# H3 block with a feed-forward branch on one Trainium2 core: another order around the first layer norms, two rows on GpSimd, another estimate for transposing transfers

## The chip, the cores and the metric

The kernel runs on one core of a Trainium2 chip. The metric is the device time of one execution, in microseconds (us). The engines of the core are named as in the profile: PE is TensorE (matmuls; PEld its weight loads), DVE is VectorE, ACT is ScalarE, POOL is GpSimd, SP is SyncE, which issues most of the transfers. Each engine works off its own queue of instructions in order; semaphores order the engines among each other.

## The reference

The input has S = 2048 rows of D = 1024 numbers; the feed-forward width is F = 3584. All inputs and the output are float32.

```python
def reference(q, k, v, shift_k, ssm_k, ssm_D, x, w1, w2):      # x of the branches is q
    xn = layernorm(q)                                          # per row, eps 1e-5
    k_shift = causal depthwise conv of k with 4 taps (shift_k)
    kv = k_shift * v
    y = irfft(rfft(kv, 2S) * rfft(ssm_k, 2S))[:S] + kv * ssm_D # per channel, over the rows
    return q + xn * y + silu(xn @ w1) @ w2
```

This is pseudocode of the reference, cut to what matters. The input `x` of its signature is not read; the two matrix products of the last term are most of the work.

## The kernel before

**Matrix products.** TensorE multiplies float16. Each float32 operand is split into a high and a low float16 part (`split`, L365): ScalarE writes the high part (L355), VectorE the low part (L347), and three matmuls per tile (high times high, high times low, low times high: L930 to L932 for the first product, L1062 to L1064 for the second) give nearly float32. The feed-forward products use a scheme with seven products of blocks in place of eight (as Strassen's): sums of blocks, named S1 to S4 for the activations and T1 to T4 for the weights, are made on VectorE ahead of the split. A few "plain" column blocks at the start (pairs 0 and 1 of w1) are done without these sums, so that TensorE has work early.

**The start.** Rows come in as 16 tiles `xt` of 128 x 1024 (128 rows of the input, one to a partition). `ln_rows` (L485) takes them in groups: tiles 0 and 1, 2 and 3, 4 to 7, then the last eight. For each group VectorE collects statistics (L497, L499), ScalarE takes a square root, VectorE forms 1/std (L503 to L507) and applies the norm in place, one `tensor_scalar` over 128 x 1024 a tile (L516). `transposes` (L527) has TensorE transpose the rows 512 columns at a time into PSUM (tile `ft`, L535), and `first_rows`, `lower_sums` (L585) and `upper_sums` make from them the operands A11, A12, A21, A22 and S1 to S4 in eight places of SBUF. `x_rows` (L623) holds this together: first the plain rows A11 and A12 of tiles 0 to 3, then A21, A22 and S1 of tiles 4 to 7 (`lower_sums`), then S2, S3, S4 (`upper_sums`). S4's place is the place in which the raw weights of pair 1 lie until they are split. In before, `x_rows` waits for the places of A22, S2, S3, S1 and S4, in this order, ahead of the first `lower_sums`.

The weights are scaled by powers of two. `scales_w1` (L706) has ScalarE sum the squares (tile `junk`), one small matmul adds them over the partitions (`norm`, L441), and VectorE forms the scales `wsc`; `factors_w1` (L747) then splits the weights into the tiles `wo`. `warm_up` (L1788) puts 26 small matmuls without a use at TensorE's start.

**The convolution.** It is done channel group by channel group (128 channels, eight groups g0 to g7), among the feed-forward matmuls. ScalarE and VectorE make `acc`, the signal k_shift * v. `signal_parts` (L1470) splits a quarter of it at a time into the tile `cm` (ring `cm_r`, one buffer, in part of the kernel also `ht`); `parts_of` (L1481) issues on SP a transposing transfer from it into the tile `hl` (helper `X`, L334). `stage1` (L1501) is the forward transform as matmuls (L1529 to L1531), ScalarE and VectorE take its result into `spec`, VectorE multiplies the spectra and does the inner transforms (tiles `spec`, `tmp`), the result is split into `zh` and `zl`, and `stage1_inv` (L1707, matmuls L1721 to L1723) transforms back. `gated` (L1729) multiplies with the normed row on VectorE into a tile `yt`, or, at the end of the kernel, into a half of a `wo` buffer, and adds it to the output in memory with two accumulating transfers that GpSimd issues (helper `G`, L339). The feed-forward results are added the same way (`out<-hf`); the last ones are written by SP.

**What sets the order.** All instructions are emitted by a planner (class `Order`, L106) while the program is built; the chip then runs fixed queues. The parts of the kernel are streams (generators) that yield operations. An operation carries its engine, an estimate of the time for which it holds the engine (`busy`), how long after that its result can be read (`late`), what it reads and writes, and a margin that is added to the time at which its operands are there. Among the next operations of all streams the planner emits the one with the least planned start less the stream's bias. Of a transfer it assumes that it ends no earlier than 3.0 us after its issue plus its bytes at 330 KB a us plus 0.2, one after the other, and no earlier than issue + busy + late. Where TensorE is planned to wait (after a planned 45 us), it emits dummy matmuls (`fill`). An activation with another function table than the one before it is charged 1.28 us. So a number in an estimate changes no operation, only the place in each engine's queue in which operations come out, and with it which buffers they get. All buffers are rings of fixed places; an operation that needs a place is emitted only when the planner has already emitted the last use of what is in it.

Of the kernel before, what the change touches and what calls it, by code (L numbers as in the profile page):

```python
# [13 lines left out]
F16 = mybir.dt.float16  # L14
I32 = mybir.dt.int32
AF = mybir.ActivationFunctionType
ALU = mybir.AluOpType
AX = mybir.AxisListType
ADD, SUB, MUL = ALU.add, ALU.subtract, ALU.mult

P = 128
# [6 lines left out]
KH = KD // 2  # L28
# [12 lines left out]
XPLACE = dict(A11=2, A12=3, A22=5, S1=0, S2=6, S3=7, S4=1)  # L41
# [64 lines left out]
class Order:  # L106
# [27 lines left out]
    def add(self, gen, bias, floor=0.0):  # L134
        s = Stream(gen, bias, floor)
        self.streams.append(s)
        self.advance(s)
# [154 lines left out]
def h3_ffn_kernel(ctx, tc, x, kp, vs, fs, shift, dskip, w1, w2, cfwd, cinv, out):  # L292
    nc = tc.nc
    ctx.enter_context(tc.manual_schedule())
    order = Order()
    add = order.add
    flag = defaultdict(Token)
# [18 lines left out]
    def V(f, o, ins, us=None, m=0.15):  # L316
        return Op("DVE", us or 1.03 * (size(o) / 960 + 0.075), 0.16, f, ins, [o], m)
# [16 lines left out]
    def X(o, i, m=0.3):  # L334

        n = size(o) * o.shape[0] * mybir.dt.size(o.dtype)
        return Op("SP", 0.6, 0.1, lambda: nc.sync.dma_start(o, i, transpose=True), [i], [o], m, n)

    def G(o, i, m=0.3):  # L339
        n = size(i) * i.shape[0] * mybir.dt.size(i.dtype)  # L340
# [135 lines left out]
    def load_row(t):  # L476
# [5 lines left out]
            yield L(xts[t][0][:, q], xr[t // T2, t % T2][:, q])  # L482
        flag["xt", t].set()

    def ln_rows():  # L485
        for t0, n, bias in ((0, 2, 0.26), (2, 2, 0.17), (4, 4, 0.15), (8, 8, 0.03)):
            yield bias
            q = slice(t0, t0 + n)
            mv = lnp.tile([P, 2, 8], F32, name="mv", bufs=2)
            m = mv[:, :, 0:n]  # L490
            order_in = (8, 9, 12, 13, 10, 11, 14, 15) if n == 8 else range(t0, t0 + n)
            for t in order_in:
                yield flag["xt", t]
                xt = xts[t][0]
                st = lnp.tile([P, 2, 6], F32, name="st", bufs=2)
                for a in range(2):
                    yield V(lambda: nc.vector.bn_stats(st[:, a, :], xt[:, a * W:(a + 1) * W]), st[:, a, :],  # L497
                            [xt[:, a * W:(a + 1) * W]], us=0.65)
                yield V(lambda: nc.vector.bn_aggr(stat[:, t, :], st), stat[:, t, :], [st], us=0.2)  # L499

            def chain(m=m, q=q):
                v = stat[:, q, 1]
                nc.vector.reciprocal(m[:, 0, :], m[:, 0, :])  # L503
                nc.vector.tensor_mul(m[:, 1, :], m[:, 0, :], m[:, 0, :])
                nc.vector.scalar_tensor_tensor(m[:, 1, :], v, 1e-5, m[:, 1, :], op0=ADD, op1=MUL)
                nc.vector.tensor_scalar(m[:, 1, :], m[:, 1, :], -0.5, 1.5, op0=MUL, op1=ADD)
                nc.vector.tensor_mul(rstd[:, q], m[:, 0, :], m[:, 1, :])  # L507
                if n == 8:
                    nc.vector.scalar_tensor_tensor(nmr, stat[:, :, 0], -1.0, rstd, op0=MUL, op1=MUL)
            yield a_act(m[:, 0, :], stat[:, q, 1], AF.Sqrt, bias=eps)  # L510
            p = V(chain, rstd[:, q], [stat[:, q, :], m[:, 0, :]], us=0.8)
            p.writes += [m[:, 0, :], m[:, 1, :]] + ([nmr] if n == 8 else [])
            yield p
            for t in order_in:
                xt = xts[t][0]
                yield V(lambda: nc.vector.tensor_scalar(xt, xt, stat[:, t, 0:1], rstd[:, t:t + 1], op0=SUB, op1=MUL),  # L516
                        xt, [xt, stat[:, t, :], rstd[:, t:t + 1]], us=0.78)
                flag["xn", t].set()

    pts = []  # L520
# [102 lines left out]
    def x_rows():  # L623
        yield from first_rows()
        second["A21"], second["tok"] = places[4].tile([P, 4, KH, 2, P], F16)
        for name in ("A22", "S2", "S3", "S1", "S4"):
            r = places[XPLACE[name]]
            yield r.ready
            xo[0][name], xtok[0][name] = r.tile([P, 4, KH, 2, P], F16)

        class Kept:
            bias = 0.14

            def __init__(self, i):
                self.i = i

            def __call__(self, name):
                if name in ("A11", "A12"):
                    return None
                o = (second["A21"] if name == "A21" else xo[0][name])[:, self.i]  # L640
                return lambda src, tok: split(o[:, :, 0], o[:, :, 1], src, XS, (tok, flag["x", 0, name]))

        yield 0.14
        half = []
        for i in range(4):
            half.append((yield from lower_sums(Kept(i), s1_r)))
        Kept.bias = 0.11
        yield 0.11
        for i in range(4):
            yield from upper_sums(Kept(i), xst_r, *half[i], t=i)  # L650

        class Spilled(Kept):
            bias = 0.02

            def __call__(self, name):
                return None if name == "A21" else lambda src, tok: spill(xsp[name][:, self.i], src, tok)

        def spill(o, src, tok):
            yield lambda: s1_r.ready() or xst_r.ready()
            r = s1_r if s1_r.ready() else xst_r  # L660
            st, stok = r.tile([P, KH, 2, P], F16)
            yield from split(st[:, :, 0], st[:, :, 1], src, XS, (tok,))
            yield L(o, st)
            stok.set()
            flag["spilled"].set()

        yield 0.02
        for i in range(4):
            part = yield from lower_sums(Spilled(i), sums_r)
            yield from upper_sums(Spilled(i), sums_r, *part)  # L670
        flag["x done"].set()
# [34 lines left out]
    def scales_w1():  # L706
        for n, (_, i) in enumerate(pairs):
            yield (0.25, 0.16, 0.1, 0.05)[min(n, 3)]
            m = 4 if n == 0 else 2
            if n >= NP:  # L710
                for a in range(m):
                    yield flag["raw", n, a]
                flag["scaled", n].set()
                continue
            yield sq_r.ready
            ss, tok = sq_r.tile([P, 4])
            for a in range(m):
                yield flag["raw", n, a]
                r = raws[n][2][a]
                yield a_act(junk[:, 0:r.shape[1]], r, AF.Square, total=ss[:, a:a + 1])  # L720

            def then(e, i=i):
                sc = wsc[:, i]
                nc.vector.tensor_scalar(sc[:, 3:5], powers[:, 3:5], e, None, op0=MUL)
                nc.vector.reciprocal(e, e)
                nc.vector.tensor_scalar(sc[:, 0:3], powers[:, 0:3], e, None, op0=MUL)
            yield from norm(ctxs["nm"], ss[:, 0:m], (m,), then, ([wsc[:, i]], [flag["scaled", n], tok]))

    spills = []

# [1067 lines left out]

    warm = lnp.tile([P, 1], F32, name="warm")
    nc.scalar.activation(warm, ones[:, 0:1], AF.Sqrt)  # L1800
    add(begin(), 0.05)
    add(warm_up(), 0.0)
    add(x_rows(), 0.03)
# [53 lines left out]
```

## Time and profile before

| | us |
|---|---|
| median of 3 runs | 1257.72 |
| lowest and highest | 1257.01, 1260.42 |
| profiled execution, its time | 1257.19 |
| profiled execution, span from the first to the last instruction | 1255.4 |
| busy: TensorE, VectorE, ScalarE, GpSimd | 1233.6, 1147.3, 731.0, 132.6 |

The mean granted clock of TensorE is 0.996. In the rows of the profile, L355 stands for all ScalarE operations of the helper `a_act`, L347 and L344 for VectorE's helpers `v_stt` and `v_tt`; so a row is read by its tiles (out<-in) rather than by its line. A row of a timeline gives the start, the duration, the engine and line, the operation with its tiles and shapes, and in brackets how long the engine was idle ahead of it and what ended that wait. A matmul's row is longer than the distance to the next one, since matmuls overlap.

### The profile page before, as it was taken

Reading aid. Unit: us, or ns where it says so; the run is one execution under the profiler, and the core shown is the slowest. Engines: PE = TensorE matmul, PEld = TensorE weight load, DVE = VectorE, ACT = ScalarE, POOL = GpSimd, SP = SyncE. Lnnn points to the kernel's source line nnn. Section 1 sums busy time; section 2 is a strip of 40 time slices with the busy share of each in tenths; the row PEclk is TensorE's granted clock in tenths of the full one; section 3 lists DMA queues with packets and bytes.
Section 4 is the critical chain, followed back from the end, with each engine's and each line's share of the span. In section 5 each row is a group of like instructions: output and inputs, shape, how many; then the busy total and the mean of one; then the engine's idle time right before and its main releaser. Section 6 shows DMA issues by size and latency. Waiting matters only on the chain.

```text
span 1255.4 us, 17118 instructions
## 1 busy us (share of the span) xinstructions
PE 1233.6 (98%) x6058; PEld 599.7 (48%) x6058; DVE 1147.3 (91%) x1517; ACT 731.0 (58%) x1165; POOL 132.6 (11%) x141
## 2 busy tenths in 40 slices
PE   7999999999999999999999999999999999899998
PEld 6544554444444544445444544544454454345444
DVE  7999997999899979999999899989989979898994
ACT  6868887878767776748752632463173264426222
POOL 0000000000000020002010300210030030113114
PEclk9999999999999999999999999999999999999999
DMA  9358889889999998879998887699597578978777
GB/s 334 94 185 293 288 297 315 285 278 325 337 335 281 264 286 262 267 224 239 352 316 209 168 270 180 147 265 263 116 220 172 129 171 245 227 157 140 163 143 92
DMA packets 254293, 292.93 MB, mean 233 GB/s; under 512 B 48768, under 2 KB 167808, under 8 KB 252032
## 3 DMA queue, kind: packets, MB, share of 16 engines
q1 hardware_dynamic: 227472, 266.93, 67.9%
q0 software_dynamic: 26736, 24.92, 15.5%
q8 instruction: 47, 0.77, 0.2%
q14 instruction: 38, 0.31, 0.1%
HBM read 193.22 MB, written 98.57 MB: 232 GB/s over the span
## 4 chain that ended last, share of the span: by engine, by line
PE 72%; DVE 9%; DMA 5%; issue 2%; ACT 1%; POOL 0%; SPq 0%; DVEq 0%; ACTq 0%; POOLq 0%
PE ff L1062 11%; PE ff L1063 11%; PE ff L1064 11%; PE ff L930 11%; PE ff L931 11%; PE ff L932 11%; DVE spec L344 3%; DMA hl<-cm 2%; PE ps L1529 2%; PE ps L1531 2%; PE ps L1530 2%; DVE x L347 1%; DMA out<-yt 1%; DVE acc L347 1%; PE ps L1723 1%
## 5 line engine op out<-in xcount | busy, mean ns | idle before, releaser
L1062 PE MATMUL ff<-x,wo 128*128 128x512 f16 x868 | 328.8, 379 | 3.8 <-ACT hf L355 3.2
L1063 PE MATMUL ff<-x,wo 128*128 128x512 f16 x868 | 328.8, 379 | 0.0
L1064 PE MATMUL ff<-x,wo 128*128 128x512 f16 x868 | 328.6, 379 | 0.0
L931 PE MATMUL ff<-x,wo 128*128 128x512 f16 (+1 forms) x808 | 303.4, 375 | 2.7 <-DVE x L347 2.7
L932 PE MATMUL ff<-x,wo 128*128 128x512 f16 (+1 forms) x808 | 303.5, 376 | 1.9 <-DVE wo L347 1.9
L930 PE MATMUL ff<-x,wo 128*128 128x512 f16 (+1 forms) x808 | 303.5, 376 | 1.5 <-ACT wo L355 1.5
L344 DVE TENSOR_TENSOR spec<-spec 128x1024 f32<-128x1024 f32 (+2 forms) x272 | 263.6, 1000 | 2.7
L1063 PEld LDWEIGHTS <-wo 128*128 128x128 f16 x868 | 85.0, 98 | 103.8 <-issue 4.8
L1064 PEld LDWEIGHTS <-wo 128*128 128x128 f16 x868 | 85.0, 98 | 102.1 <-issue 0.8
L1062 PEld LDWEIGHTS <-wo 128*128 128x128 f16 x868 | 85.9, 99 | 99.8 <-issue 0.8
L932 PEld LDWEIGHTS <-wo 128*128 128x128 f16 x808 | 79.2, 98 | 98.0 <-issue 3.4
L930 PEld LDWEIGHTS <-wo 128*128 128x128 f16 x808 | 80.7, 100 | 88.8 <-ACT wo L355 1.7
L931 PEld LDWEIGHTS <-wo 128*128 128x128 f16 x808 | 79.3, 98 | 87.6
L355 ACT ACTIVATE hf<-ff,invc 128x512 f32<-128x512 f32 x60 | 40.9, 683 | 114.2 <-PE ff L1064 89.4
L341 POOL DMA_DIRECT2D out<-hf x59 | 51.8, 879 | 468.5 <-ACT hf L355 429.5
L341 POOL DMA_DIRECT2D out<-yt x56 | 62.2, 1274 | 321.0 <-DVE yt L347 186.3
L344 DVE TENSOR_TENSOR tmp<-spec 128x2048 f32<-128x2048 f32 (+1 forms) x48 | 92.5, 1933 | 1.0
L355 ACT ACTIVATE spec<-spec 128x1024 bf16<-128x1024 f32 x32 | 33.7, 1054 | 73.2 <-DVE spec L344 73.1
L347 DVE SCALAR_TENSOR_TENSOR ht<-hf,wsc,ht 128x1024 f16<-128x1024 f32 (+1 forms) x56 | 67.3, 1202 | 8.4 <-ACT ht L355 8.2
L347 DVE SCALAR_TENSOR_TENSOR acc<-kin,taps,acc 128x1024 f32<-128x1024 f32 x48 | 61.4, 1279 | 4.4 <-ACT acc L355 4.3
L355 ACT ACTIVATE spec<-ps 128x512 f32<-128x512 f32 x96 | 55.6, 590 | 15.2 <-PE ps L1531 11.4
L355 ACT ACTIVATE ht<-hf,wsc 128x1024 f16<-128x1024 f32 (+1 forms) x56 | 60.8, 1086 | 5.9 <-DVE hf L344 2.2
(173 smaller groups left out, 1756.6 us busy)
## 6 DMA issues: line engine op xcount, KB each, us to landing
wo<-hs SPq DMA_DIRECT2D x160, 256.0 KB, 3.6
hs<-ht SPq DMA_DIRECT2D x80, 256.0 KB, 4.7
wraw<-in_w SPq DMA_DIRECT2D x31, 512.0 KB, 5.5
out<-hf POOLq DMA_DIRECT2D x59, 256.0 KB, 4.4
raw<-in_w SPq DMA_DIRECT2D x28, 512.0 KB, 5.6
kin<-in_kp SPq DMA_DIRECT2D x16, 704.0 KB, 5.9
kf<-in_fs SPq DMA_DIRECT2D x8, 1024.0 KB, 6.0
hsfS<-ht SPq DMA_DIRECT2D x32, 256.0 KB, 4.2
```

Of the source, the lines that this page charges most:

```text
L341: return Op("POOL", 1.1, 4.8, lambda: nc.gpsimd.dma_start(o, i, accum_op=ADD), [i], [o], m, n)
L344: return V(lambda: nc.vector.tensor_tensor(o, a, b, op=op), o, [a, b], **k)
L347: return V(lambda: nc.vector.scalar_tensor_tensor(o, a, s, b, op0=op0, op1=op1), o, [a, b] + ([] if isinstance(s, float) else [s]), **k)
L355: nc.scalar.activation(o, i, func, scale=scale, **kw)
L930: nc.tensor.matmul(o, w[:, 0, k], xf[:, :, k, 0], start=first and k == 0, stop=False, **kw)
L931: nc.tensor.matmul(o, w[:, 0, k], xf[:, :, k, 1], start=False, stop=False, **kw)
L932: nc.tensor.matmul(o, w[:, 1, k], xf[:, :, k, 0], start=False, stop=last and k == KH - 1, **kw)
L1062: nc.tensor.matmul(o, hx[:, n, 0, :], wc[:, n, 0, q], start=first and n == 0, stop=False, **kw)
L1063: nc.tensor.matmul(o, hx[:, n, 0, :], wc[:, n, 1, q], start=False, stop=False, **kw)
L1064: nc.tensor.matmul(o, hx[:, n, 1, :], wc[:, n, 0, q], start=False, stop=last and n == 3, **kw)
L1529: nc.tensor.matmul(o, cf[:, 0], hi[i], start=i == 0, stop=False, **kw)
L1530: nc.tensor.matmul(o, cf[:, 0], lo[i], start=False, stop=False, **kw)
```

## The change

It has five parts.

1. The helper `X` of the transposing transfers has a `late` of 6.0 in place of 0.1: the planner takes them to end 6.6 us after the issue or later.
2. Tiles 6 and 7 of the layer norm are applied by GpSimd (`LNPOOL`), planned at 1.3 + 0.3 us, with the same operation; the other tiles stay with VectorE.
3. `x_rows` takes S4's place only after the four `lower_sums`, ahead of the `upper_sums`; the other four places are taken as before.
4. The margin of the matmul in `norm` is 0.3 in place of 1.5 for the first pair of weights.
5. The planner starts with the square root's table as the one that is loaded, so the first root is not charged 1.28 us.

```diff
     def X(o, i, m=0.3):
...
-        return Op("SP", 0.6, 0.1, lambda: nc.sync.dma_start(o, i, transpose=True), [i], [o], m, n)
+        return Op("SP", 0.6, 6.0, lambda: nc.sync.dma_start(o, i, transpose=True), [i], [o], m, n)
...
+    LNPOOL = (6, 7)
+
     def ln_rows():
...
-                yield V(lambda: nc.vector.tensor_scalar(xt, xt, stat[:, t, 0:1], rstd[:, t:t + 1], op0=SUB, op1=MUL),
-                        xt, [xt, stat[:, t, :], rstd[:, t:t + 1]], us=0.78)
+                def apply(e):
+                    return lambda: e.tensor_scalar(xt, xt, stat[:, t, 0:1], rstd[:, t:t + 1], op0=SUB, op1=MUL)
+                ins = [xt, stat[:, t, :], rstd[:, t:t + 1]]
+                if t in LNPOOL:
+                    yield Op("POOL", 1.3, 0.3, apply(nc.gpsimd), ins, [xt], 0.3)
+                else:
+                    yield V(apply(nc.vector), xt, ins, us=0.78)
...
-        for name in ("A22", "S2", "S3", "S1", "S4"):
-            r = places[XPLACE[name]]
-            yield r.ready
-            xo[0][name], xtok[0][name] = r.tile([P, 4, KH, 2, P], F16)
+
+        def have(*names):
+            for name in names:
+                r = places[XPLACE[name]]
+                yield r.ready
+                xo[0][name], xtok[0][name] = r.tile([P, 4, KH, 2, P], F16)
+
+        yield from have("A22", "S2", "S3", "S1")
...
             half.append((yield from lower_sums(Kept(i), s1_r)))
+        yield from have("S4")
         Kept.bias = 0.11
...
-            yield from norm(ctxs["nm"], ss[:, 0:m], (m,), then, ([wsc[:, i]], [flag["scaled", n], tok]))
+            yield from norm(ctxs["nm"], ss[:, 0:m], (m,), then, ([wsc[:, i]], [flag["scaled", n], tok]), 0.3 if n == 0 else 1.5)
...
     nc.scalar.activation(warm, ones[:, 0:1], AF.Sqrt)
+    order.table = AF.Sqrt
```

In the program that comes out, the operations are those of before but for the two applied rows (VectorE two fewer, GpSimd two more), five dummy matmuls fewer, and some other buffers.

## Prediction

> **What bounds the kernel now.** I read the page's totals first, then TensorE's own waits, then each wait's cause.
>
> ```profile
> span 1255.4 us, 17118 instructions
> PE 1233.6 (98%) x6058; PEld 599.7 (48%) x6058; DVE 1147.3 (91%) x1517; ACT 731.0 (58%) x1165; POOL 132.6 (11%) x141
> PE   7999999999999999999999999999999999899998
> ...
> POOL 0000000000000020002010300210030030113114
> ```
>
> TensorE is busy 98% of the span. The change takes no real matmul away, so time can only come out of the idle 1255.4 − 1233.6 = 21.8 us, out of stretches at a lower clock, and out of the last transfers. Where the idle time lies shows in the table by stage (columns: window, length, TensorE, weight loads, VectorE, ScalarE, GpSimd, granted clock, DMA share, GB/s) and in TensorE's timeline (start, duration, line, and in brackets the wait ahead of it and what released it):
>
> ```profile
> 10.00:20.00 10.00, 4.86 (x32) 3.66 (x32) 9.29 (x21) 8.39 (x19) 0.00 (x0) 0.87 1.04 391
> 20.00:30.00 10.00, 8.27 (x70) 6.93 (x69) 9.04 (x24) 7.08 (x14) 0.00 (x0) 0.96 1.06 377
> 30.00:40.00 10.00, 8.63 (x64) 6.09 (x63) 9.55 (x26) 9.85 (x15) 0.00 (x0) 1.00 0.18 46
> 40.00:50.00 10.00, 9.75 (x52) 4.97 (x50) 10.00 (x16) 8.99 (x18) 0.00 (x0) 1.00 0.53 168
> 50.00:60.00 10.00, 8.68 (x51) 5.31 (x52) 9.96 (x18) 8.40 (x14) 0.00 (x0) 1.00 0.34 105
> 60.00:100.00 40.00, 40.00 (x188) 18.26 (x187) 39.43 (x72) 25.76 (x36) 0.00 (x0) 1.00 0.57 191
> ```
> ```profile
> 17.82 0.39 PE L932 MATMUL ff<-x,wo 128*128 128x256 f16 x1 [1.14 <-DVE wo L347]
> 54.55 0.38 PE L931 MATMUL ff<-x,wo 128*128 128x512 f16 x1 [1.09 <-DVE x L347]
> 700.56 0.38 PE L1529 MATMUL ps<-hl,cfw 128*128 128x512 f16 x1 [1.72 <-ACT tmp L355]
> 1092.58 0.58 PE L1062 MATMUL ff<-x,wo 128*128 128x512 f16 x1 [3.17 <-ACT hf L355]
> ```
>
> From 10 to 60 us TensorE lacks 5.14 + 1.73 + 1.37 + 0.25 + 1.32 = 9.8 us, and VectorE is 90 to 100% busy there: VectorE paces the start. After 54.55 TensorE is covered; from 60 to 100 it has no idle time. Of the later waits, 1.72 us at 700.56 and 3.17 us at 1092.58 are the large ones.
>
> The one at 1092.58 goes back to a transposing transfer:
>
> ```profile
> 1079.93 10.67 DMA hl<-cm
> ```
> ```profile
> 1090.62 0.72 ACT L355 ACTIVATE cm<-acc,csc 128x512 f16<-128x512 f32 x1 [4.37 <-DMA hl<-cm]
> 1091.86 1.24 ACT L355 ACTIVATE hf<-ff,invc 128x512 f32<-128x512 f32 x2
> ```
> ```profile
> DMA to landing us min/median/max: 3.0/4.6/10.7
> ```
> ```profile
> 1095.94 0.39 PE L1064 MATMUL ff<-x,wo 128*128 128x512 f16 x1
> 1096.39 0.38 PE L1063 MATMUL ff<-x,wo 128*128 128x512 f16 x1
> ```
> ```profile
> 1092.00:1100.00 8.00, 7.42 (x27) 3.01 (x27) 8.00 (x12) 3.13 (x5) 1.57 (x2) 0.79 0.64 163
> ```
>
> The first row is the chain of waits, the next two ScalarE's timeline, the fourth the tile cm (fastest, median and slowest of 31 transfers), the fifth and sixth TensorE's timeline. There is one cm buffer. The next half split into it waits in ScalarE's queue until the transfer has landed; the eviction hf stands behind it in the same queue; TensorE waits for a place that this eviction frees. After the gap eight matmuls start within 1095.94 − 1092.58 = 3.36 us, at a granted clock of 0.79 in that window. At the pace of the two rows at 1095.94 and 1096.39 (two starts in 0.45 us) they take 1.8. So the event costs 3.17 + 1.6 = 4.8 us.
>
> **The change part by part.** Terms are made against the profiled execution's 1257.19 us, 0.5 below the median 1257.72.
>
> *The estimate of the transposing transfer, 0.1 to 6.0.* No instruction is added. The planner now believes a landing at 6.6 us after the issue, not at about 4.0 (3.0, 0.8 for 256 KB, 0.2), so it puts the next cm split later in ScalarE's queue. I counted, in the order that each built program has, the matmuls between a transfer's issue and the point where TensorE needs the eviction that stands behind the next cm split. At 0.22 us for 512 columns that was 9.5 to 11.7 us in the tightest places of before and is 14 us or more everywhere in the changed order. The slowest transfer took 10.7. The event goes: **−4.8**. Its bounds are 0 (a transfer takes longer than 14) and −4.8.
>
> What is late next? In each conv group VectorE must finish the spectra between the last forward eviction and the first inverse part, while TensorE works off FFN matmuls.
>
> ```profile
> 598.38:697.84 99.46, 99.46 (x466) 45.38 (x464) 97.61 (x112) 48.25 (x80) 8.34 (x9) 1.00 0.96 284
> 1032.39:1135.40 103.01, 99.83 (x459) 45.15 (x458) 98.36 (x126) 42.06 (x74) 11.22 (x13) 0.98 0.84 207
> ```
> ```profile
> 697.84 2.19 ACT L355 ACTIVATE zh<-spec,csc 128x1024 f16<-128x1024 f32 x2 [5.99 <-DVE spec L347]
> ```
> ```profile
> 1032.39 0.69 DVE L344 TENSOR_TENSOR spec<-spec,ps 128x512 f32<-128x512 f32 x1 [3.83 <-ACT spec L355]
> ```
>
> The two stretches are those of groups 2 and 6, from the first VectorE work on the last forward tiles to the first inverse part (zh). In group 2 VectorE works 97.61 of 99.46 us and is late: ScalarE waits 5.99 us for it, and 1.72 of that reaches TensorE at 700.56. Counting each operation of the stretch by the duration of its own row, group 2 has 98.2 us of VectorE work beside 104.3 us of matmuls in before and 96.4 beside 101.7 in the changed order: a slack of 6.1 becomes 5.3, so up to 0.8 more at that gap; I take **+0.8**, bounds 0 and 0.8. Group 6 had 98.4 beside 105.6, and the gap at 1092.58 gave VectorE 4.8 more; now it has 99.6 beside 104.3, a slack of 4.7. VectorE itself idled 3.83 at that stretch's start. Group 2 lost 1.72 at a slack of 6.1, so a slack of 4.7 would lose 1.72 + 1.4 = 3.1 by that row, and 0 if the wait for ScalarE at the start of the stretch shrinks. Against that, group 7 had a slack of 5.1 in before and no such wait. Between these, with bounds of 0 and 4, I take **+1.8**. The other groups' slacks change by at most 1.3 us, and none falls below 5.1.
>
> *Start: margin, first table, S4's place, two rows on GpSimd.* In the built order the matmul that sums the first weight norm now comes before the second transposition, so the first factor's scale is there about 1.3 us earlier and the first FFN stream starts near 16.4 instead of 17.82. But squares on ScalarE then stand ahead of the root for rows 2 and 3, and their norm comes about 1.3 us later, so most of that is lost again at TensorE near 25 and 30 us. What counts is when VectorE gets through:
>
> ```profile
> 36.16 2.98 DVE L516 TENSOR_SCALAR xt<-xt,stat,rstd 128x1024 f32<-128x1024 f32 x4
> 50.69 0.68 DVE L344 TENSOR_TENSOR raw<-raw,raw 128x512 f32<-128x512 f32 x1
> 51.40 0.69 DVE L344 TENSOR_TENSOR raw<-raw 128x512 f32<-128x512 f32 x1
> 53.81 1.28 DVE L347 SCALAR_TENSOR_TENSOR x<-ft,x 128x512 f16<-128x512 f32 x2
> ```
> ```profile
> 1.02 0.29 POOL masks.py:199 TENSOR_SCALAR_AFFINE_SELECT ident<-ident 128x128 f32<-128x128 f32 x1
> ```
>
> Rows 4 to 7 were applied in 2.98 us, 0.74 each, ending at 39.1. Now VectorE applies rows 4 and 5 alone, from about 37.4 (1.3 later) to 38.85: −0.2. S4's place is no longer waited for ahead of the lower sums; in the built order the two sums of raw weights (0.68 + 0.69, less overlap 1.3) fall behind the splits that TensorE waits for at 54.55. That wait ends near 53.0: −0.2 − 1.3 = **−1.5**. Bounds: −2.5 (the earlier stream is kept) and +1 (the later norm of rows 2 and 3 adds a wait that nothing gives back). From 60 us on, the built order keeps at least 2.5 us of VectorE lead, where it was 1.3, so the gain isn't lost there. Dummy matmuls fall from 10 to 5, in time that TensorE waits anyway: nothing.
>
> The two applies on GpSimd: no row shows this operation there. The nearest is the select over 128 columns, 0.29 us; eight times the columns bound it by 2.3 us. The lower bound is VectorE's 0.74. I take 2.3, by the GpSimd row. TensorE needs rows 6 and 7 near 45.5 and 49.5, and GpSimd can begin near 37.4 with nothing queued: in the page's 40 slices, quoted above, it first works in the fifteenth, past 440 us. So 8 us for the first and 6 for each of two are free: 0. [...]
>
> What speaks against the move is that both engines would work at once on SBUF, with VectorE 100% busy from 40 to 50 us. No row of before shows GpSimd computing beside VectorE, so I bound it: nothing at best; at worst VectorE stands still for both, 2 × 2.3 = 4.6. The nearest rows are GpSimd's transfer issues, with a VectorE row beside them and one without:
>
> ```profile
> 1233.67 3.34 POOL L341 DMA_DIRECT2D out<-wo  x3 [1.90 <-DVE wo L347]
> ```
> ```profile
> 1235.32 0.75 DVE L347 SCALAR_TENSOR_TENSOR wo<-ps,csc,xg 128x512 f32<-128x512 f32 x1
> ```
> ```profile
> 39.06 0.74 DVE L347 SCALAR_TENSOR_TENSOR wo<-x,wsc,wo 128x512 f16<-128x512 f32 x1
> ```
>
> Beside the issues VectorE takes 0.75 us, without them 0.74. By these rows I take 0, and keep 4.6 as a rival. [...]
>
> *The end.*
>
> ```profile
> 1246.23 1.11 POOL L341 DMA_DIRECT2D out<-wo  x1
> 1248.68 0.88 POOL L341 DMA_DIRECT2D out<-wo  x1 [1.34 <-ACT wo L355]
> ```
> ```profile
> 1250.11 1.73 SPq L332 DMA_DIRECT2D out<-hf  x2
> ```
> ```profile
> out<-wo POOLq DMA_DIRECT2D x8, 128.0 KB, 3.4
> out<-hf SPq DMA_DIRECT2D x2, 128.0 KB, 3.2
> ```
>
> SP's last transfer ends its issue at 1251.84 and lands 3.2 later, which with its completion gives 1255.4. GpSimd's last, issued at 1248.68, is done well before. In the changed order the last conv group stands 5.8 us later (its last inverse matmul 7.2 instead of 13.0 us before TensorE's end). Its eight accumulating transfers, 1.1 us of GpSimd each, come later; two gated tiles take wo halves which the two before them still send out, and VectorE's last two evictions queue behind one of them. From the evictions and the landing that it waits for I place the start of the last such issue at 1251.9 to 1253.9, against an unmoved end of TensorE. With 3.4 to land and the 0.4 that SP's last has behind its landing (1255.4 − 1251.84 − 3.2) the end is 1255.7 to 1257.7, or 1.1 more if landing counts from the issue's end: +0.3 to +3.4. I take the middle of the first pair, **+1.3**.
>
> Sum: −4.8 + 0.8 + 1.8 − 1.5 + 1.3 = −2.4, so 1257.19 − 2.4 = **1254.8 us**. Its own range: the bounds do not all fall together; 1252 to 1258.
>
> **Rivals.** (1) VectorE doesn't bind in groups 2 and 6: −4.8 − 1.5 + 1.3 = −5.0, **1252.2**. For it: TensorE lacks 3.18 us in group 6's row above, which is the gap at 1092.58 and nothing else, and group 7 did without a wait at 5.1. Against: that gap had given VectorE 4.8.
>
> (2) The change doesn't do what it says: a transfer still holds cm longer than the queue allows, there or at another eviction. −1.5 + 0.8 + 1.3 = +0.6, **1257.8**. For it: landings go from 3.0 to 10.7 by what else the DMA engines carry. Against: 14 us of matmuls.
>
> ```profile
> 700.77 0.38 PE L1530 MATMUL ps<-hl,cfw 128*128 128x512 f16 x1
> ```
>
> (3) Slower: VectorE comes so late to the first inverse parts of groups 2 and 6 that TensorE's wait drops its clock in both. This decides once such a wait nears 3.2 us: after the 1.72 at 700.56 the next matmul starts 0.21 later (700.77), after the 3.17 at 1092.58 matmuls stand 0.42 apart (3.36 over eight). Each wait then costs 4.8: −4.8 − 1.5 + 1.3 + 9.6 = +4.6, **1261.8**. For it: slacks of 5.3 and 4.7. Against: it needs VectorE about 1.5 us later still in group 2. [...]
>
> (4) GpSimd's two applies hold VectorE up: +4.6 on the forecast, **1259.4**.
>
> **How the numbers follow.** About 0.3%, 3.8 us, is what a measurement of this kernel can tell from no change: faster is below 1253.9, slower above 1261.5. Chances: forecast 0.42, (1) 0.27, (2) 0.13, (3) 0.11, (4) 0.07. Faster: nearly all of (1) and a third of the forecast, 0.25 + 0.14 = 0.39. Slower: half of (3) and some of the ends of (2) and (4), where another eviction joins them, 0.10. Between: 0.51. The range runs from (1) with the start's better bound to past (4): 1250.5 to 1260.5; what it leaves out is most of (3) and the tails.
>
> **What would show it.** No TensorE wait of 3 us near 1090 and no ScalarE wait of over 4 us on hl<-cm with an eviction behind it (term −4.8); the last wait of the start near 53.0 and VectorE's L516 group in six rows there; zh of group 2 and 6 waiting 6 us or more for VectorE with a TensorE gap of 2 to 3 us (+0.8, +1.8); a last transfer issued by GpSimd after SP's (+1.3); rows of some 2 us for GpSimd's L516 or its replacement, with VectorE's rows beside them of unchanged length. A new wait over 2 us in an FFN eviction of groups 0 to 5 would make the sum wrong.

## The result and the profile after

| | before | changed |
|---|---|---|
| median, us | 1257.42 (6 runs) | 1263.14 (6 runs) |
| lowest and highest | 1256.28, 1260.42 | 1261.16, 1265.73 |
| profiled execution, its time | 1257.19 | 1262.95 |
| its span | 1255.4 | 1261.2 |
| start of TensorE's last matmul | 1250.68 | 1252.85 |
| from there to the end of the span | 4.72 | 8.35 |

The ratio is 1.0048, interval 1.0031 to 1.0066: slower by half a per cent. The profiled executions differ by 5.76 us, their spans by 5.8. Of the spans' difference, 2.17 lie ahead of the start of TensorE's last matmul and 3.63 behind it. The page of the changed kernel has fewer busy microseconds on TensorE, VectorE and ScalarE than before:

```profile
span 1261.2 us, 17102 instructions
PE 1231.9 (98%) x6048; PEld 597.8 (47%) x6048; DVE 1145.2 (91%) x1515; ACT 730.7 (58%) x1165; POOL 141.3 (11%) x143
```

So the loss is in waits and in the end. TensorE's timeline, the larger waits from 53 us on and the last matmul:

```profile
53.61 0.38 PE L943 MATMUL ff<-x,wo 128*128 128x512 f16 x1 [0.57 <-DVE x L347]
...
165.24 0.63 PE L542 MATMUL ft<-ident,xt 128*128 128x128 f32 x4 [0.66 <-DVE pow L457]
...
446.87 0.38 PE L1541 MATMUL ps<-hl,cfw 128*128 128x512 f16 x1 [1.13 <-DVE tmp L344]
...
529.43 0.49 PE L327 MATMUL ff<-one,zero 128*128 128x128 f32 x2 [0.67 <-DVE hf L344]
...
703.71 0.38 PE L1541 MATMUL ps<-hl,cfw 128*128 128x512 f16 x1 [2.45 <-ACT tmp L355]
...
1087.73 0.38 PE L1074 MATMUL ff<-x,wo 128*128 128x512 f16 x1 [0.64 <-ACT ff L355]
...
1102.25 0.38 PE L1074 MATMUL ff<-x,wo 128*128 128x512 f16 x1 [1.41 <-DVE hf L347]
...
1145.64 0.27 PE L1734 MATMUL ps<-zl,civ 128*128 128x256 f16 x1 [0.90 <-DVE zl L347]
...
1156.82 0.38 PE L1541 MATMUL ps<-hl,cfw 128*128 128x512 f16 x1 [0.70 <-DVE tmp L344]
...
1252.85 0.27 PE L1076 MATMUL ff<-x,wo 128*128 128x256 f16 x1
```

(In this kernel L942 to L944 and L1074 to L1076 are the feed-forward matmuls, L1541 to L1543 the forward, L1733 to L1735 the inverse transform.) The wait of 3.17 us at 1092.58 is gone, with the low clock behind it (from 1092 to 1100 the granted clock is 1.00 where it was 0.79). Smaller waits stand in its place, most of them for VectorE. The row at 529.43 is a dummy matmul that waits for an eviction itself (a dummy matmul has two records in the profile, so x2 is one of them: with five dummies fewer the page has 10 matmul records fewer, 6048 where before has 6058).

What was late next, once the event near 1092 was gone, are two other transfers. The first row below is ScalarE's: an eviction waits 2.59 us for a transfer `out<-hf`, and the work on `ff` that releases TensorE at 1087.73 stands right behind it. The other rows are VectorE's: it waits 2.21 us for a load of weights, and the eviction for which TensorE waits 1.41 at 1102.25 stands behind that in VectorE's queue, with no other wait between.

```profile
1086.50 0.69 ACT L355 ACTIVATE hf<-ff,invc 128x512 f32<-128x512 f32 x1 [2.59 <-DMA out<-hf]
```
```profile
1088.79 0.69 DVE L344 TENSOR_TENSOR x<-wraw,x 128x512 f32<-128x512 f32 x1 [2.21 <-DMA wraw<-in_w]
...
1101.45 0.75 DVE L347 SCALAR_TENSOR_TENSOR hf<-ff,invc,hf 128x512 f32<-128x512 f32 x1
```

The end, in GpSimd's and SyncE's timelines of the changed kernel and then in the table by stage, first of it, then of before (the last two figures of a row are the DMA engines' share and GB/s):

```profile
1239.88 2.22 POOL L341 DMA_DIRECT2D out<-wo  x2 [4.63 <-DVE wo L347]
1243.30 2.20 POOL L341 DMA_DIRECT2D out<-wo  x2 [1.20 <-DVE wo L347]
...
1248.80 4.33 POOL L341 DMA_DIRECT2D out<-wo  x4
1254.85 2.22 POOL L341 DMA_DIRECT2D out<-wo  x2 [1.72 <-issue]
```
```profile
1252.28 1.73 SPq L332 DMA_DIRECT2D out<-hf  x2
```
```profile
1253.00:1258.00 5.00, 0.12 (x2) 0.00 (x0) 0.48 (x1) 0.00 (x0) 2.35 (x3) 0.73 1.22 193
```
```profile
1253.00:1255.40 2.40, 0.00 (x0) 0.00 (x0) 0.00 (x0) 0.00 (x0) 0.00 (x0) 0.50 0.10 32
```

In before the DMA engines have nearly nothing left to do after 1253 (share 0.10, 32 GB/s); in the changed kernel they are full until 1258 (share 1.22, 193 GB/s). Of the last convolution group's eight accumulating transfers the first four are issued by 1245.5; the other four come among the feed-forward's last ones. SyncE's own last transfers, in the same crowd, take 5.0 us to land where they took 3.2:

```profile
out<-hf SPq DMA_DIRECT2D x2, 128.0 KB, 5.0
```

The two rows on GpSimd, and VectorE beside them:

```profile
36.93 8.43 POOL L519 TENSOR_SCALAR xt<-xt,stat,rstd 128x1024 f32<-128x1024 f32 x2 [35.62 <-DVE rstd L509]
```
```profile
36.85 2.34 DVE L519 TENSOR_SCALAR xt<-xt,stat,rstd 128x1024 f32<-128x1024 f32 x2
...
40.97 0.73 DVE L347 SCALAR_TENSOR_TENSOR wo<-x,wsc,wo 128x512 f16<-128x512 f32 x1
...
42.22 1.09 DVE L347 SCALAR_TENSOR_TENSOR wo<-x,wsc,wo 128x512 f16<-128x512 f32 x1
```

GpSimd takes 4.2 us a row. VectorE's two rows beside it take 2.34 where two of the four of before took 1.49, and one split takes 1.09 where its like takes 0.73: VectorE, freed of 1.49, loses 1.2 of it. In the two runs below with all rows on VectorE its four rows take 2.98 again and these splits 0.74 or 0.75.

### The profile page after: what moved, and what is told of

Read it like the earlier page. It is cut to its first block, busy times and chain, and to the rows that moved or that the text cites. A ratio compares the mean times of both kernels' runs of the same rounds, so it can differ in the third digit from the quotient of the medians.

```text
span 1261.2 us, 17102 instructions
## 1 busy us (share of the span) xinstructions
PE 1231.9 (98%) x6048; PEld 597.8 (47%) x6048; DVE 1145.2 (91%) x1515; ACT 730.7 (58%) x1165; POOL 141.3 (11%) x143
## 4 chain that ended last, share of the span: by engine, by line
PE 68%; DVE 18%; DMA 6%; issue 4%; ACT 4%; SPq 0%; POOL 0%; POOLq 0%; DVEq 0%; ACTq 0%
PE ff L943 10%; PE ff L942 10%; PE ff L944 10%; PE ff L1074 10%; PE ff L1076 10%; PE ff L1075 10%; DVE spec L344 5%; DVE tmp L344 3%; DMA wraw<-in_w 3%; DVE x L347 2%; PE ps L1541 2%; PE ps L1542 1%; PE ps L1543 1%; DMA hsfA<-ht 1%; DVE spec L347 1%
## 5 line engine op out<-in xcount | busy, mean ns | idle before, releaser
L1074 PE MATMUL ff<-x,wo 128*128 128x512 f16 x868 | 328.1, 378 | 2.6 <-DVE hf L347 2.0
L1076 PE MATMUL ff<-x,wo 128*128 128x512 f16 x868 | 328.1, 378 | 0.0
L942 PE MATMUL ff<-x,wo 128*128 128x512 f16 (+1 forms) x808 | 303.5, 376 | 0.4 <-ACT x L355 0.2
L944 PE MATMUL ff<-x,wo 128*128 128x512 f16 (+1 forms) x808 | 303.6, 376 | 0.0
L1076 PEld LDWEIGHTS <-wo 128*128 128x128 f16 x868 | 84.9, 98 | 101.6
L1074 PEld LDWEIGHTS <-wo 128*128 128x128 f16 x868 | 85.8, 99 | 99.6
L944 PEld LDWEIGHTS <-wo 128*128 128x128 f16 x808 | 79.3, 98 | 95.7 <-issue 3.6
L942 PEld LDWEIGHTS <-wo 128*128 128x128 f16 x808 | 80.8, 100 | 87.2
```

The source lines that it names most:

```text
L942: nc.tensor.matmul(o, w[:, 0, k], xf[:, :, k, 0], start=first and k == 0, stop=False, **kw)
L944: nc.tensor.matmul(o, w[:, 1, k], xf[:, :, k, 0], start=False, stop=last and k == KH - 1, **kw)
L1074: nc.tensor.matmul(o, hx[:, n, 0, :], wc[:, n, 0, q], start=first and n == 0, stop=False, **kw)
L1076: nc.tensor.matmul(o, hx[:, n, 1, :], wc[:, n, 0, q], start=False, stop=last and n == 3, **kw)
```

## The experiments

Theory A: the estimate of 6.0 brings both the gain (the event near 1092) and the loss (a later last group, and VectorE late). Theory B, the rival: the parts at the start, GpSimd's rows at their head, cost the time. "Tail" is the time from the start of TensorE's last matmul to the end of the span. Ratios are to the kernel before, which was measured beside each version; its median lay between 1256.4 and 1258.9, so ratios are compared and not medians.

**The estimate alone.** Edit, to the kernel before:

```diff
-        return Op("SP", 0.6, 0.1, lambda: nc.sync.dma_start(o, i, transpose=True), [i], [o], m, n)
+        return Op("SP", 0.6, 6.0, lambda: nc.sync.dma_start(o, i, transpose=True), [i], [o], m, n)
```

> The kernel before with only the estimate of the transposing transfer at 6.0; everything at the start is as before. Theory A (the estimate sets both the gain and the loss): TensorE's wait of 3.2 us near 1092 is gone (-4.8), the last convolution group stands 5.8 us nearer to the end, so GpSimd issues the last accumulating transfers after SyncE's last and the span ends some 8 us after TensorE instead of 4.5 (+3.6), and new waits of TensorE at forward and inverse transforms add 2 to 6; about 1261 in all. Theory B (the parts at the start, with GpSimd's two rows at their head, cost the time): the tail and the convolution's waits are those of before, and with the gap near 1092 gone the time is 1253 or less.

Measured: ratio 1.0028 (1.0012 to 1.0045). GpSimd's and TensorE's timelines:

```profile
1254.34 2.22 POOL L341 DMA_DIRECT2D out<-wo  x2 [2.00 <-issue]
```
```profile
1100.88 0.38 PE L1062 MATMUL ff<-x,wo 128*128 128x512 f16 x1 [1.09 <-DVE hf L347]
...
1156.02 0.38 PE L1529 MATMUL ps<-hl,cfw 128*128 128x512 f16 x1 [1.29 <-DVE tmp L344]
...
1252.05 0.27 PE L1064 MATMUL ff<-x,wo 128*128 128x256 f16 x1
```

The span is 1260.6, so the tail is 8.55. Most of the same waits, a us or so earlier or later, and the same tail as in the changed kernel, with the start of before: theory A. B is out as the main cause. Whether the parts at the start add to the loss isn't told, since the intervals of 1.0028 and 1.0048 overlap. The waits near 700 differ: 0.83 at 701.40 and 1.04 at 716.67, where the changed kernel has 2.45 in one.

**The start alone.** Edit, to the changed kernel:

```diff
-        return Op("SP", 0.6, 6.0, lambda: nc.sync.dma_start(o, i, transpose=True), [i], [o], m, n)
+        return Op("SP", 0.6, 0.1, lambda: nc.sync.dma_start(o, i, transpose=True), [i], [o], m, n)
```

> The changed kernel with the estimate of the transposing transfer back at 0.1; the four parts at the start stay. Theory A: the tail is that of before (SyncE issues the last transfer, 4.5 us from TensorE's end to the span's), a wait of 2 to 4 us on a transposing transfer is back, and the start's 0.9 us is all that stays of a difference: 1256 to 1257.5. Theory B: the loss stays, 1261 or more.

Measured: ratio 0.9998 (0.9982 to 1.0013). The event near 1092 is back:

```profile
1092.06 0.58 PE L1074 MATMUL ff<-x,wo 128*128 128x512 f16 x1 [3.42 <-ACT hf L355]
```

The tail is 5.26 (span 1255.3, last matmul at 1250.04). The four parts at the start together move nothing that these runs can tell.

**All groups but group 1.** In the orders that come out with the estimate switched on for one group at a time, the last inverse transform stands 7.2 us of matmuls ahead of TensorE's end with group 1 alone, and 13.0 with any other group alone (orders that were built; of these only group 7 alone ran). Edit, to the changed kernel:

```diff
-    def X(o, i, m=0.3):
+    def X(o, i, m=0.3, late=6.0):
...
-        return Op("SP", 0.6, 6.0, lambda: nc.sync.dma_start(o, i, transpose=True), [i], [o], m, n)
+        return Op("SP", 0.6, late, lambda: nc.sync.dma_start(o, i, transpose=True), [i], [o], m, n)
...
-                    yield X(x[:, 0].rearrange("p f s w -> p (f s) w"), c.rearrange("p f s w -> p (f s w)"))
+                    yield X(x[:, 0].rearrange("p f s w -> p (f s) w"), c.rearrange("p f s w -> p (f s w)"), late=0.1 if g == 1 else 6.0)
```

> The changed kernel, but the estimate of 6.0 holds for the transposing transfers of all channel groups except group 1, which have 0.1. In the order that comes out the last inverse transform stands 13.0 us of matmuls ahead of TensorE's end, as before, not 7.2. Theory A: the tail is 4.5 us again, so 3.6 less than the changed kernel has, and the wait near 1092 stays away: 1258 to 1260 or better. Theory B: as the changed kernel within 1.5 us, 1261.5 to 1264.5.

Measured: ratio 0.9956 (0.9939 to 0.9973), at the fast end of what was expected. One channel group's estimate makes the difference between slower and faster:

```profile
span 1253.0 us, 17100 instructions
```
```profile
1246.17 0.88 POOL L341 DMA_DIRECT2D out<-wo  x1 [1.34 <-ACT wo L355]
```

TensorE's last matmul starts at 1248.17, the tail is 4.83. The waits at 529, 1102, 1145 and 1156 are gone as well. Counted in matmuls between the first forward matmul of a group and TensorE's end, the changed order is later than this one by 0.6 us in group 2, not at all in group 3, by 1.9 in group 4, 2.6 in groups 5 and 6, 4.5 in group 7 and 5.8 at its last inverse matmul. How group 1's estimate comes to the end is not shown: group 3 is not late, and in the run with 5.0, below, group 2 is as late as in the changed kernel (694.3 us of matmuls ahead of the end in both), and the end is good.

**All rows on VectorE.** Edit, to the changed kernel:

```diff
-    LNPOOL = (6, 7)
+    LNPOOL = ()
```

> The changed kernel with all rows of the layer norm applied by VectorE. Theory A: GpSimd's 8.4 us for the two rows lie beside other work and cost nothing in the end; the tail is as in the changed kernel (the last inverse transform stands 7.2 us ahead of TensorE's end here too), time within 2 us of it, 1261 to 1265. Theory B: faster than the changed kernel by 2 us or more, 1257 to 1261.

Measured: ratio 1.0029 (1.0015 to 1.0044), tail 8.75 (span 1260.2, last matmul at 1251.45). As theory A expects, but not cleanly: the order differs, with nine dummy matmuls (18 records) in one place near 248 us. The run with group 7 alone and all rows on VectorE, below, shows what they cost.

**Group 7 alone, with the new start, and with the old.** Edits: as for group 1, to the changed kernel and to the kernel before, with this in the call:

```diff
-late=0.1 if g == 1 else 6.0)
+late=6.0 if g == 7 else 0.1)
```

> The changed kernel with the estimate of 6.0 for group 7 alone, the group whose transfer holds cm near 1080 to 1090. If that one group's order is what removes the 4.8 us, the event is gone and the rest is as with the start's parts alone (which was 0.6 us ahead of before at TensorE's end): 1251.5 to 1253.5 against 1257.2. If the other groups' new order is needed too, a wait of 2 to 4 us near 1090 stays and the time is 1255 to 1257.5.

> The kernel before with the estimate of 6.0 for group 7 alone, the least edit of all. The event near 1092 goes and nothing else moves ahead of it: -4.8 us less what new wait comes in its place, 0.9960 to 0.9980 of before. If the event stays or moves, 0.999 to 1.001.

Measured: 0.9958 (0.9942 to 0.9974) and 0.9977 (0.9965 to 0.9989). In both the event is gone; the one group whose transfers hold `cm` there is enough. In the second, at equal matmul work against before, TensorE is 0.4 us late shortly ahead of the event and 4.6 early behind it: it gives back 5.0, close to the 4.8 worked out. The matmuls of the second run come in the same order as in before, so this is the cleanest trial of that price.

**The kernel before, all groups but group 1.** Edit, to the kernel before: as in the run with all groups but group 1.

> The kernel before with the estimate of 6.0 for the transposing transfers of all groups but group 1; the start is that of before. The wait near 1092 is gone, the tail is 4.7 us. If the estimate for the right groups is all that is gained, the time is that of the run with the new start (0.9956 of before), within 1 us; if the parts at the start help, it is 0.5 to 1.5 us longer; if they harm, shorter by as much.

Measured: 0.9966 (0.9953 to 0.9979), against 0.9956 (0.9939 to 0.9973) with the new start. The intervals overlap: again nothing that the parts at the start are worth can be told.

**5.0 in place of 6.0.** Edit, to the changed kernel:

```diff
-        return Op("SP", 0.6, 6.0, lambda: nc.sync.dma_start(o, i, transpose=True), [i], [o], m, n)
+        return Op("SP", 0.6, 5.0, lambda: nc.sync.dma_start(o, i, transpose=True), [i], [o], m, n)
```

> The changed kernel with 5.0 in place of 6.0 in the estimate, for all groups. The built order has the last inverse transform 13.0 us ahead of TensorE's end, as before. Theory A: the tail is 4.7 us, no wait of over 2 us near 1090, and the time is that of the orders with a good tail, 1252 to 1255. If 6.0 as such (later transfers for everybody) were the cause of the loss, 5.0 would give most of it too: 1259 or more.

Measured: 0.9967 (0.9956 to 0.9979), median 1251.67. Page, TensorE's timeline and the tile cm:

```profile
span 1249.5 us, 17099 instructions
```
```profile
712.86 0.38 PE L1541 MATMUL ps<-hl,cfw 128*128 128x512 f16 x1 [0.50 <-DVE yt L347]
...
1244.31 0.27 PE L1076 MATMUL ff<-x,wo 128*128 128x256 f16 x1
```
```profile
DMA to landing us min/median/max: 3.0/5.0/8.3
```

After 713 TensorE has no wait of 0.1 us or more but 0.57 at the very end. The tail is 5.2. So neither a late estimate as such nor the transfers' real time (a median of 5.0 us from issue to landing here, 4.6 in the changed kernel) is what lost: 5.0 and 6.0 mean the same to the chip and differ only in the order that falls out. This version, like those with group 1 or all groups but 7 left out, beats both kernels; among them the runs don't rank.

**GpSimd by itself.** Edit, to the changed kernel with group 7 alone: two more applies, on a tile that nobody reads, ahead of everything.

```diff
+    alone = hts.whole[0]
+    nc.vector.memset(alone, 1.0)
+    for _ in range(2):
+        nc.gpsimd.tensor_scalar(alone, alone, zero, one, op0=SUB, op1=MUL)
     add(begin(), 0.05)
```

> The kernel with the estimate of 6.0 for group 7 alone, and ahead of everything two more applies of the same form (128x1024 float32, one input, two scalars) on a tile that nobody reads, on GpSimd, when VectorE is idle or collects statistics. In the changed kernel the two rows took 4.1 and 4.3 us beside a busy VectorE. Theory E (GpSimd needs 4 us for such a row whatever VectorE does): the first of the two takes about 4.1. Theory F (it was held up by VectorE): the first takes 2.3 us or less, as worked out in the prediction from the select's row.

Measured:

```profile
2.28 7.66 POOL L1817 TENSOR_SCALAR ht<-ht,zero,one 128x1024 f32<-128x1024 f32 x2 [0.97 <-DVE ht L1815]
```

3.83 us a row while VectorE idles or collects statistics, 4.2 beside a busy one: theory E. The row is slow by itself; VectorE adds a tenth.

**Group 7 alone, all rows on VectorE.** Edit: `LNPOOL = ()`, as above, in the changed kernel with group 7 alone.

> The kernel with the estimate of 6.0 for group 7 alone and all rows applied by VectorE: GpSimd's part taken out, now in an order whose tail is good. If the two rows on GpSimd help, it is slower than with them (1252.9, 0.9958 of before) by 1 us or more; if they cost, faster by 1 or more; if the 1.2 us that VectorE lost beside GpSimd just cancels the 1.5 that it was freed of, within 1 us at the start, and any other difference comes from the order after 60 us.

Measured: ratio 1.0011 (1.0000 to 1.0023). This order does not compute the reference's result, and why is not known. So the run tells only where time goes, and the run with all rows on VectorE above, which does compute it, stands beside it. At equal matmul work TensorE is 1.5 us ahead of before when the start is over, where the same kernel with the rows on GpSimd was 0.6 ahead (in the run above it is 1.2 ahead, where the changed kernel is 0.9). Then one row loses it:

```profile
248.33 4.21 PE L327 MATMUL ff<-one,zero 128*128 128x128 f32 x18 [3.23 <-DVE hf L344]
```
```profile
252.00:254.00 2.00, 2.00 (x7) 0.88 (x7) 0.59 (x1) 1.62 (x2) 0.00 (x0) 0.51 0.82 202
```

The planner believed in a wait there and filled it with nine dummy matmuls (18 records), which themselves waited 3.2 us; with their 4.2 that is 7.4 of the 8.2 us that it falls behind there. The rest goes in the first matmuls behind them, at a granted clock of 0.51 (second row). The run above has the same wait of 3.23 us there, at 248.63. So the two rows on GpSimd don't help the start, if anything they cost 0.3 to 0.9; what they did was to give an order without these dummies.

**What in the tail takes the time.** Four versions of the changed kernel, each with a part of the last channel group's accumulating transfers left out or altered. The edits, in the order of the expectations:

```diff
-                yield G(out4[b][:, :, t, g * P:(g + 1) * P], yt[:, b])
+                if (g, t) != (NG - 1, TO[-1]):
+                    yield G(out4[b][:, :, t, g * P:(g + 1) * P], yt[:, b])
...
+                n = P if g < NG - 1 else P // 2
+                yield G(out4[b][:, :, t, g * P:g * P + n], yt[:, b, :, 0:n])
...
+                if g < NG - 1:
+                    yield G(out4[b][:, :, t, g * P:(g + 1) * P], yt[:, b])
...
+                if g < NG - 1:
+                    yield G(out4[b][:, :, t, g * P:(g + 1) * P], yt[:, b])
+                else:
+                    yield G(out4[b][:, 0, t, 2 * P * (g // 2):2 * P * (g // 2 + 1)], yt[:, b].rearrange("p i w -> p (i w)"))
```

> The changed kernel without the two accumulating transfers of the very last gated tile (that part of the output is not added); the order on all other engines is the same. If the tail of 8.3 us from TensorE's last matmul to the end is these transfers', SyncE's last transfer ends the span again, 4.7 to 5.5 us after the last matmul. If something else holds the end, it stays at 7 us or more.

> The changed kernel, but the accumulating transfers of the last channel group carry 64 of its 128 channels (the rest of that group is not added to the output): the same number of issues and pieces, half the bytes. Theory C (the DMA engines need the time for the bytes): the tail shrinks from 8.3 to 6.5 us or less, and GpSimd's wait ahead of its last two issues of 1.7 us goes. Theory D (what counts is the number of issues and pieces, in GpSimd's queue or in the DMA engines): the tail stays at 7.5 us or more.

> The changed kernel without the eight accumulating transfers of the last channel group (that group is not added to the output). From TensorE's last matmul to the end of the span it was 8.4 us in the changed kernel, 7.5 without the last two of these transfers, 6.8 with half their bytes, and 4.7 in before. If the lateness of this group's eight transfers is the whole of the longer tail, it is 4.5 to 5.2 us now; if the feed-forward's own accumulating transfers are late too, 5.5 or more.

> The changed kernel, but the accumulating transfers of the last channel group write rows of 1024 bytes in place of two pieces of 512 (to other columns and rows than they should: the output of that group is misplaced): the same issues and bytes, half the pieces. If the DMA engines' time for a piece sets the drain, the tail falls from 8.4 to 7 us or less; if the bytes set it, or GpSimd's issues, it stays at 7.8 or more. Half the bytes in as many pieces had given 6.8.

| | span | last matmul | tail |
|---|---|---|---|
| changed | 1261.2 | 1252.85 | 8.35 |
| last tile's two transfers left out | 1256.9 | 1249.38 | 7.5 |
| half the bytes in all eight | 1260.1 | 1253.27 | 6.8 |
| all eight left out | 1256.7 | 1251.57 | 5.1 |
| half as many pieces, the same bytes | 1261.7 | 1253.91 | 7.8 |

The page and TensorE's last row of the run with all eight left out, from which such a line of the table is read:

```profile
span 1256.7 us, 17088 instructions
```
```profile
1251.57 0.27 PE L1076 MATMUL ff<-x,wo 128*128 128x256 f16 x1
```

The first expectation missed: without the last two transfers the tail does not drop to 5, since two more of the group still come among the feed-forward's last ones and the DMA engines stay full (share 1.16 from 1249.4 to 1253.4). With all eight gone it is 5.1, near before's 4.7, so this group is all but the whole of it. Half the bytes take back 1.5 of the 3.2 us, which is about half; half the pieces take back 0.6, which brings the tail just to the 7.8 that I had set as the least for the bytes or the issues, and is less than the 0.72 us by which one wait of one order differed between executions (last section). That run also speaks against GpSimd's issues. Its last ones, and the landing of the very last:

```profile
1251.91 3.54 POOL L341 DMA_DIRECT2D out<-wo  x4 [0.47 <-ACT wo L355]
```
```profile
out<-wo POOLq DMA_DIRECT2D x1, 128.0 KB, 6.8
```

They end at 1255.45, 1.5 us after the start of the last matmul, where the changed kernel's end 4.2 after it. Yet the tail is only 0.6 shorter: the last transfer, issued sooner, takes 6.8 us to land. So the bytes weigh most (theory C). With half of them GpSimd's wait ahead of its last issues only fell from 1.7 to 1.3 us; what it waits for there stays open. Each of these is one execution.

## Why the prediction was wrong

1254.8 was forecast, 1263.1 came. In the profiled executions −2.4 was to be +5.8, so 8.2 us are to be accounted for. Progress is compared at equal matmul work, from TensorE's timelines.

1. **The event near 1092, −4.8: the mechanism was right, the net −2.6.** The two runs with group 7 alone confirm price and cause. But the step "what is late next" looked only at the inverse transforms. Two other transfers stood right there: ScalarE's wait of 2.59 for `out<-hf` gave TensorE 0.64, and VectorE's wait of 2.21 for a load of weights gave it 1.41 (with small change 2.2 us against the sum). Before had 1.04 of that wait on weights, which did not reach TensorE; with group 7 alone, new start and old, it is 0.3 and nothing. Why it is longer in the changed order is not shown.
2. **The end, +1.3: +3.6.** The cause was the one named, the last group 5.8 us later. The place of the last issue was forecast well: it began at 1255.6 (first row below), 1253.4 against an unmoved TensorE, within 1251.9 to 1253.9 and 0.5 behind the middle. The size failed behind it: from the issue's start to the end I priced 3.4 + 0.4 = 3.8, and it took 5.6. In the crowd of the last transfers it took 4.2 to land (second row), not 3.4. And the 0.4 was misread: 3.2 is the median of SyncE's last two transfers of before, and the very last, begun at 1251.5, landed in 2.6 (third row), 1.3 ahead of the span's end; here it was 1.4. So 0.5 + 0.8 + 1.0 (2.3 us).

```profile
L341 POOL DMA_DIRECT2D out<-wo x2: 1083/1294/1506, 1254.8 to 1255.6; - x2
```
```profile
out<-wo POOLq DMA_DIRECT2D x1, 128.0 KB, 4.2
```
```profile
out<-hf SPq DMA_DIRECT2D x1, 128.0 KB, 2.6
```

3. **The start, −1.5: −0.9 at 54 us, 0 by 250 us.** The last wait of the start ends at 53.61, near the 53.0 forecast; then 0.66 at 165.24, where before lost nothing, and smaller things use it up. That the 2.5 us of lead after 60 us would keep it was wrong. The run of the start alone came out at 0.9998 (1.5 us).
4. **Groups 0, 1 and 3, priced at nothing: about +2.3.** I wrote that the other groups' slacks change by at most 1.3 us and concluded no wait. TensorE lost 0.6 near 447, 1.2 near 529 (0.67, and a dummy matmul, of which I had said that they cost nothing) and 0.5 near 820. Waits of this size come and go with the order: the kernel before with all groups but group 1 has 1.38 at 817.29 and none near 529.
5. **Groups 2 and 6, +0.8 and +1.8: the sizes were right, in part by luck.** At 703.71 the wait is 2.45 where it was 1.72. Behind the event it was 0.90 at 1145.64 and 0.70 at 1156.82, with small change 1.9. It came at the second part of group 6's inverse and at the next forward matmul, though, not at the first inverse part, and 1.8 was a choice between 0 and 4. Group 2's wait is 0.83 in the run with the estimate alone, so the 2.45 can't be put down to the estimate alone.
6. **GpSimd's rows, 0: nothing at the end, by another sum.** 4.2 us a row, not 2.3; they ended at 45.36, just in time. VectorE was held up beside them, as rival 4 has it, but by 1.2 us (2.34 where 1.49 and 1.09 where 0.73), not 4.6; what the two engines hold each other up by is not shown.

The misses of items 1 to 4 add up to 8.3. Rival 3 named the slower side with the wrong mechanism: behind the 2.45 us at 703.71 the next matmuls stand 0.22 apart, at a granted clock of 1.00. It dropped behind longer waits: 3.17 in before (0.79 from 1092 to 1100), 3.42 with the event back (the next matmuls 0.43 apart, later 0.22), and 3.23 ahead of the dummies near 248 (0.51 from 252 to 254). In the rest of before and of the changed kernel it is 1.00 from 60 to 1250 us. The step that failed as a whole was to take the built order's shift of the last group as one term at the end. Every group from 4 on stood later in that order, and waits elsewhere had to be priced anew. The run with all groups but group 1 has none of the waits at 447, 529, 1102, 1145 and 1156 and not the tail, so they come with this order; which lateness makes which wait is not shown.

## What to carry to other kernels

In a kernel whose order a planner writes, an estimate is a lever on the order first and a statement on the chip second: change it for the one place where the trace shows the wait, and look in the built order at everything that shifts, above all at what stands last. Price an end at which several transfers come late as a backlog of the DMA engines, not as one landing (here their share was 1.22 from 1253 to 1258, and landings took 4.2 and 5.0 us where before had 3.4 and 3.2), and read from the last transfer itself, not from a median, what follows its landing. And ask of a removed stall not only which wait of the same kind is next, but what each engine's queue has right behind it.

## What the runs showed that I had not expected

- One GpSimd `tensor_scalar` over 128 x 1024 float32 takes 3.83 us with VectorE nearly idle, five times VectorE's 0.74, and more than the 2.3 us worked out from the 0.29 of a select over 128 columns.
- GpSimd's two rows, 8.4 us, and VectorE's work beside them were both longer: 0.8 us on one VectorE row and 0.35 on one split, and 4.2 us for a GpSimd row in place of 3.83.
- Eight accumulating transfers of 128 KB near the end cost 3.2 us of tail and go with a median landing of SyncE's last two transfers of 5.0 us, where it is 3.6 with the eight left out.
- Executions of one order differ by most of a us in single waits: with the same order up to there, the kernel before waited for nothing near 227 us, before with all groups but group 1 0.72, before with the estimate alone 0.30.
